# A planned order worked out anew: sigmoid attention and a gated feed-forward layer on one core

## The chip, the cores and the metric

The kernel runs on one core of a Trainium2 chip. The metric is the time of one execution on the device in microseconds (us); a comparison takes the median of several executions.

The core has five engines that run side by side: TensorE (PE in the profile) does matrix products into PSUM, ScalarE (ACT) activation functions, VectorE (DVE) elementwise work, copies and 32x32 block transposes, GpSimd (POOL) here only issues the loads, and SyncE (SP) issues the output stores. Each engine runs its own list of instructions strictly in the order in which the program wrote them, and waits at the first one whose operands or buffers are not ready.

## The reference

```python
def _attn_ref(q, k, v):                     # 8 batches, 12 heads, 448 tokens, 64 wide
    scores = scale * np.matmul(q, k.transpose(0, 1, 3, 2)) - np.log(S)
    attn = 1.0 / (1.0 + np.exp(-scores))    # a sigmoid, no softmax
    return np.matmul(attn, v).astype(np.float32)

def _moe_ref(x, w_in, w_out, beta):         # x: 3584 tokens x 768; w_in: 768 x 2048; w_out: 2048 x 768
    h = x @ w_in
    g = h * (1.0 / (1.0 + np.exp(-beta * h)))
    return (g @ w_out).astype(np.float32)
```

Attention runs per head; the heads of a batch, side by side, are the 768 columns of `x`. Inputs and output are float32; the kernel computes in float16 with float32 sums.

## The kernel before

The work is cut into **tasks**, each a few instructions of one engine. A task has a name, and the names are what the change is written in:

- **Loads (POOL queue, lines 778 to 806).** The 12 heads of a batch make three groups of four heads, 24 groups in all. `q7.0.0` and `k7.0.0` are the queries and keys of group 7 (224 KB each in SBUF) and go to one of three `raw` buffers; `v3.0` to `v3.5` are six parts of the values of batch 3 (four of 144 KB, two of 48 KB) and go to one of two `v` buffers. `wi0` to `wi7` and `wo00` to `wo11` are the weights. Loads also turn float32 into float16.
- **DVE transposes and copies.** `tq` and `tk` (L818 and L832) turn a group's raw queries and keys into `qT` and `kT` (four buffers each), and the `raw` buffer is free once they are done. `vv3` (L797) copies the two small parts of a batch's values to the other partitions.
- **Scores (PE, L845).** `h0.0.1` and the like for the first three groups, by halves of the queries; `s12.2` for group 12, key block 2. Each is followed on ACT by two sigmoids (L855) into one of ten `attn` buffers.
- **Values (PE, L867).** `a12.0.0` multiplies the sigmoids of group 12 with `v` of batch 4 (group number over three, rounded down). DVE copies the result to `xT` (L877). The last group of a batch frees its `v` buffer, and the load that takes it next waits for that: `v3.0` for `a8.0.0`, `v5.0` for `a11.0.0`, `v6.0` for `a14.0.0`, `v7.0` for `a17.0.0`; all loads behind it in `LOAD_ORDER` wait with it.
- **First layer (PE, L883).** `d3.14.0` makes 128 of the 2048 hidden columns for the 448 tokens of batch 3 in six matmuls; batch 0 does it by halves. ACT takes the sigmoid with `beta` (L892, three `sg` buffers), and DVE multiplies (`gt`, L901) and so frees the PSUM bank.
- **Second layer (PE, L1003).** `t5.3.1` is the second half of product 3 of the seven (a Strassen-like scheme) that make a pair of 128-token tiles; DVE forms sums of operands (`sum`) and adds up the results in `osb`; `z5.1` and `z5.0` (SP, L1035) store the two tiles of the pair, 384 KB each, in pieces of 96 KB for most.

What order these tasks have on their engines is worked out by the program itself before any of it is issued. `plan` (line 523) steps through time with a cost for each task. PE and POOL take their tasks in the order of two long strings, `PE_ORDER` (line 668) and `LOAD_ORDER` (line 699). DVE, ACT and SP have no such string: at line 655 the planner gives them, whenever they are free, the ready task that has been ready longest:

```python
t = min(cand, key=lambda t: (ready_at[t.i] - t.soon, t.i))
```

So a transpose stands in DVE's list at the place where the planner believed its load to be done. A load's due time is reckoned at lines 640 to 642: all loads pass one after the other through one queue at the load's own rate (195 KB/us for a whole group's queries or keys, 187 and 133 for parts of the values), 1.83 us after their issue at the earliest, and are done 0.1 us after the last byte. Stores have the fixed cost (1.7, 3.4) and are no part of that queue.

On the chip, the lists are fixed: nothing is reordered when a load comes at another time than planned. The waits between engines are semaphores.

Of the kernel before, what the change touches and what calls it, by code (L numbers as in the profile page):

```python
# [665 lines left out]


PE_ORDER = """
i0 h1.0.1 h1.0.0 h2.0.1 h2.0.0 h0.0.00 h0.0.1 h0.0.01 a1.0.0 a1.0.1 h2.1.0 a0.0.0 a0.0.1 h0.1.0 a2.0.0 a2.0.1 h0.1.1
h2.1.1 d0.9.0 d0.4.0 h1.1.1 d0.8.0 a0.1.0 h1.1.0 a2.1.0 a0.1.1 s3.1 a1.1.0 a1.1.1 s3.0 a2.1.1 d0.10.0 d0.11.0 d0.5.1  # L670
s3.2 d0.7.1 d0.2.0 d0.6.0 d0.7.0 s3.3 d0.0.1 d0.5.0 s4.1 a3.0.0 s4.2 d0.1.1 d0.2.1 d0.9.1 d0.15.0 s4.0 d0.11.1 d0.14.0
d0.1.0 d0.14.1 s4.3 d0.6.1 d0.12.0 s5.0 a4.0.0 s5.1 d0.10.1 d0.3.0 d0.13.1 s5.2 d0.12.1 d0.8.1 d0.13.0 d0.3.1 a5.0.0
d0.4.1 d0.0.0 d0.15.1 d1.6.0 d1.7.0 d1.0.0 d1.1.0 d1.10.0 d1.2.0 d1.8.0 d1.15.0 d1.12.0 d1.4.0 d1.11.0 d1.5.0 d1.14.0
t0.0.0 t0.0.1 t0.1.0 t0.1.1 t0.2.0 t0.2.1 s6.0 t0.3.0 t0.3.1 d1.9.0 s6.1 t0.4.0 d1.3.0 d1.13.0 t0.4.1 s6.2 t0.5.0
t0.5.1 t0.6.0 s6.3 t1.0.0 t1.0.1 s7.2 t0.6.1 a6.0.0 s7.0 t1.1.0 t1.1.1 t1.2.0 t1.2.1 s7.1 t1.3.0 t1.3.1 t1.4.0 t1.4.1
t1.5.0 s8.1 t1.5.1 a7.0.0 s8.0 t2.0.0 t2.0.1 t1.6.0 s8.2 t1.6.1 t2.1.0 t2.1.1 t2.2.0 t2.2.1 t2.3.0 s8.3 t2.3.1 t2.4.0
t2.4.1 t2.5.0 a8.0.0 s10.0 t2.5.1 t2.6.0 t2.6.1 s9.0 d2.1.0 d2.2.0 d2.7.0 s9.1 d2.4.0 d2.0.0 d2.3.0 s9.2 d2.5.0
d2.15.0 d2.13.0 d2.10.0 d2.12.0 d2.9.0 d2.8.0 d2.11.0 d2.6.0 d2.14.0 a9.0.0 s10.2 t3.0.0 t3.0.1 t3.1.0 s10.1 t3.1.1
t3.2.0 t3.2.1 t3.3.0 t3.3.1 t3.4.0 t3.4.1 s10.3 t3.5.0 t3.5.1 t3.6.0 t3.6.1 t4.0.0 t4.0.1 s11.1 a10.0.0 t4.1.0 t4.1.1
s11.0 t4.2.0 t4.2.1 t4.3.0 t4.3.1 s11.2 t4.4.0 t4.4.1 t4.5.0 t4.5.1 s12.2 a11.0.0 t4.6.0 s12.0 t4.6.1 d3.9.0 s12.1  # L680
d3.14.0 d3.12.0 d3.0.0 d3.10.0 s13.0 d3.8.0 d3.6.0 s12.3 d3.15.0 d3.1.0 s13.2 a12.0.0 d3.3.0 d3.5.0 d3.4.0 s13.1
d3.11.0 d3.13.0 s14.2 d3.7.0 d3.2.0 s14.1 a13.0.0 t5.0.0 t5.0.1 t5.1.0 s14.0 t5.1.1 t5.2.0 t5.2.1 t5.3.0 t5.3.1 s14.3
t5.4.0 t5.4.1 a14.0.0 s15.0 t5.5.0 t5.5.1 t5.6.0 t5.6.1 d4.2.0 d4.10.0 s15.2 d4.7.0 d4.4.0 s15.1 d4.8.0 d4.13.0 d4.6.0
s16.0 d4.12.0 a15.0.0 s17.2 d4.14.0 d4.0.0 s16.1 t6.0.0 t6.0.1 t6.1.0 s16.2 d4.3.0 d4.1.0 d4.11.0 d4.15.0 t6.1.1
d4.5.0 d4.9.0 t6.2.0 t6.2.1 t6.3.0 t6.3.1 s16.3 t6.4.0 t6.4.1 t6.5.0 t6.5.1 a16.0.0 s17.1 t7.0.0 t7.0.1 t7.1.0 t6.6.0
t6.6.1 s17.0 t7.1.1 t7.2.0 t7.2.1 t7.3.0 t7.3.1 s18.2 t7.4.0 t7.4.1 a17.0.0 s18.1 t7.5.0 t7.5.1 t7.6.0 d5.8.0 s19.0
t7.6.1 d5.14.0 s18.3 d5.15.0 d5.11.0 d5.12.0 d5.9.0 d5.4.0 s18.0 d5.0.0 d5.5.0 d5.1.0 a18.0.0 s19.2 d5.2.0 d5.13.0
s19.1 d5.7.0 d5.3.0 s20.3 d5.6.0 d5.10.0 s20.0 a19.0.0 t8.0.0 t8.0.1 t8.1.0 s20.2 t8.1.1 t8.2.0 t8.2.1 t8.3.0 t8.3.1
s20.1 t8.4.0 t8.4.1 s21.1 t8.5.0 t8.5.1 a20.0.0 s21.2 t8.6.0 t8.6.1 s22.2 d6.1.0 d6.12.0 d6.13.0 s21.0 d6.10.0 d6.0.0
d6.7.0 d6.14.0 d6.2.0 a21.0.0 s22.1 d6.6.0 d6.3.0 s22.3 d6.15.0 d6.4.0 d6.5.0 d6.9.0 s22.0 d6.8.0 t9.0.0 s23.2 a22.0.0  # L690
t9.0.1 t9.1.0 t9.1.1 t9.2.0 s23.1 t9.2.1 t9.3.0 t9.3.1 t9.4.0 t9.4.1 d6.11.0 s23.0 t9.5.0 t9.5.1 t9.6.0 t10.0.0
t10.0.1 t10.1.0 a23.0.0 t10.1.1 t10.2.0 t10.2.1 t10.3.0 t10.3.1 t10.4.0 t11.0.0 d7.2.0 t9.6.1 d7.5.0 d7.3.0 d7.10.0
t10.4.1 t10.5.0 t11.0.1 t10.5.1 t10.6.0 t10.6.1 d7.4.0 d7.1.0 d7.0.0 d7.7.0 d7.11.0 d7.6.0 t11.1.0 t11.1.1 d7.8.0
t11.2.0 d7.13.0 d7.12.0 d7.9.0 t11.2.1 t11.3.0 t11.3.1 d7.14.0 t11.4.0 d7.15.0 t11.4.1 t11.5.0 t11.5.1 t11.6.0 t11.6.1
t12.0.0 t12.0.1 t12.1.0 t12.1.1 t12.2.0 t13.0.0 t12.2.1 t13.0.1 t13.1.0 t12.3.0 t12.3.1 t13.1.1 t12.4.0 t12.4.1
t12.5.0 t12.5.1 t13.2.0 t13.2.1 t12.6.0 t13.3.0 t12.6.1 t13.3.1 t13.4.0 t13.4.1 t13.5.0 t13.5.1 t13.6.0 t13.6.1
"""
# [395 lines left out]
```

## Time and profile before

| | us |
|---|---|
| median of 3 runs | 403.95 (403.72 to 404.39) |
| the profiled execution | 401.18 |
| its span, first to last instruction | 399.4 |
| PE busy (share of the span) | 381.7 (96%) |
| ACT busy | 241.7 (61%) |
| DVE busy | 236.3 (59%) |
| POOL busy (issuing loads) | 69.1 (17%) |

The mean granted clock of TensorE is 0.972. The profiled execution ran 2.77 us shorter than the median of the timed ones, and 1.78 us of it lie outside the span.

A line of a timeline reads: start and length in us, engine, source line, operation, output and inputs, count, and in brackets how long the engine stood idle just before and what it waited for. A line of the waits reads: who waited for whom, us in total, how many times, the longest.

### The profile page before, as it was taken

To read this page: it belongs to the slowest core of one execution; us is meant where nothing else is said; L and a number is where in the kernel's file an instruction comes from. 1 tells how busy PE (TensorE), PEld (TensorE's weight loads), DVE (VectorE), ACT (ScalarE), POOL (GpSimd) and SP (SyncE) were. 2 spreads that over 40 slices of the span, in tenths; PEclk is the share of its full clock that TensorE was granted. 3 is DMA by queue.
4 is the path that set the end of the run, shared out by engine and by line. 5 is a ranking of instruction groups with operands and counts; after the bars stand their busy time and mean duration, and the time that the engine had idled before them with its cause. 6 is when DMAs were issued, how large, how long until landed. Compare 5 with 4: busy or idle time off the path is not lost.

```text
span 399.4 us, 7347 instructions
## 1 busy us (share of the span) xinstructions
PE 381.7 (96%) x2958; PEld 191.9 (48%) x2958; DVE 236.3 (59%) x456; ACT 241.7 (61%) x331; POOL 69.1 (17%) x117
## 2 busy tenths in 40 slices
PE   6899999999996999997999999988999999999996
PEld 2456765544452445442444445433444445555563
DVE  2445659995663566545587538534585445465755
ACT  1999995477645654685865874476967784135100
POOL 7845307120023000071020010070000000000000
PEclk9589999999999999998999999999999999999999
DMA  8999999655139302199054041396003000140114
GB/s 111 154 197 196 204 203 160 98 89 119 41 56 202 40 2 47 39 189 166 0 94 97 3 54 30 74 169 117 0 2 81 1 2 3 38 102 18 35 45 158
DMA packets 42289, 34.30 MB, mean 86 GB/s; under 512 B 21888, under 2 KB 38672, under 8 KB 42256
## 3 DMA queue, kind: packets, MB, share of 16 engines
q0 software_dynamic: 37008, 22.81, 41.6%
q1 hardware_dynamic: 5248, 11.02, 10.5%
q8 instruction: 23, 0.38, 0.4%
q14 instruction: 10, 0.08, 0.1%
HBM read 45.62 MB, written 11.01 MB: 142 GB/s over the span
## 4 chain that ended last, share of the span: by engine, by line
PE 84%; DMA 8%; ACT 3%; DVE 2%; issue 2%; POOL 1%; DVEq 0%; POOLq 0%
PE ps L883 33%; PE ps L1003 32%; PE ps L867 10%; PE ps L845 10%; DMA v<-in_v_dram 3%; DMA raw<-in_k_dram 3%; ACT attn L855 2%; DMA raw<-in_q_dram 2%; POOL v L789 1%; DVE gt L901 1%; DVE kT L832 0%; ACT sg L892 0%; POOL v L793 0%; DVE qT L818 0%; DVE osb L901 0%
## 5 line engine op out<-in xcount | busy, mean ns | idle before, releaser
L855 ACT ACTIVATE attn<-ps,nlogs 128x896 f16<-128x896 f32 (+1 forms) x171 | 160.0, 1002 | 61.6 <-PE ps L845 59.5
L883 PE MATMUL ps<-xT,w_in 128*128 128x448 f16 (+1 forms) x864 | 157.1, 335 | 8.6 <-DVE gt L901 8.1
L892 ACT ACTIVATE sg<-ps,beta_sb 128x448 f32<-128x448 f32 (+1 forms) x144 | 82.2, 606 | 63.6 <-PE ps L883 49.8
L883 PEld LDWEIGHTS <-w_in 128*128 128x128 f16 x864 | 82.2, 98 | 79.5 <-issue 24.7
L901 DVE TENSOR_TENSOR gt<-ps,sg 128x448 f16<-128x448 f32 (+1 forms) x144 | 78.3, 566 | 66.4 <-ACT sg L892 66.1
L1003 PEld LDWEIGHTS <-sum 128*128 128x128 f16 x560 | 52.7, 98 | 42.8 <-issue 9.1
L901 DVE TENSOR_TENSOR sum<-gt 128x1024 f16<-128x1024 f16 x70 | 47.5, 686 | 38.5 <-PE ps L1003 37.5
L1003 PE MATMUL ps<-w_T,sum 128*128 128x384 f16 x336 | 60.9, 327 | 0.0
L845 PE MATMUL ps<-qT,kT 32*128 32x448 f16 (+3 forms) x864 | 55.7, 358 | 3.7 <-DVE kT L832 2.5
L867 PE MATMUL ps<-attn,v 128*64 128x448 f16 (+3 forms) x432 | 43.9, 349 | 0.3 <-ACT attn L855 0.3
L901 DVE TENSOR_TENSOR osb<-ps,osb 128x384 f32<-128x384 f32 x70 | 38.5, 551 | 7.6 <-PE ps L1003 6.7
L1003 PE MATMUL ps<-w_out,gt 128*128 128x384 f16 x224 | 41.1, 327 | 0.0
L1003 PE MATMUL ps<-w_out,sum 128*128 128x384 f16 x224 | 40.2, 326 | 0.0
L877 DVE CAST xT<-ps 128x448 f16<-128x448 f32 (+1 forms) x54 | 28.5, 559 | 18.8 <-PE ps L867 18.7
L789 POOL DMA_DIRECT2D v<-in_v_dram x32 | 20.3, 642 | 110.1 <-PE ps L867 105.4
L867 PEld LDWEIGHTS <-v 128*64 128x64 f16 (+1 forms) x432 | 19.8, 110 | 26.9 <-issue 19.6
L845 PEld LDWEIGHTS <-kT 32*128 32x128 f16 (+1 forms) x864 | 14.8, 100 | 32.4 <-issue 27.2
L1003 PEld LDWEIGHTS <-gt 128*128 128x128 f16 x224 | 20.7, 98 | 17.6 <-issue 4.9
L778 POOL DMA_DIRECT2D raw<-in_q_dram x28 | 15.6, 565 | 59.3 <-DVE qT L818 56.6
L832 DVE STREAM_TRANSPOSE kT<-raw 128x384 f32<-128x384 f32 (+3 forms) x50 | 18.7, 388 | 11.7 <-DMA raw<-in_k_dram 11.6
L818 DVE STREAM_TRANSPOSE qT<-raw 128x448 f32<-128x448 f32 (+2 forms) x28 | 17.1, 610 | 7.5 <-DMA raw<-in_q_dram 7.5
L778 POOL DMA_DIRECT2D raw<-in_k_dram x25 | 14.0, 560 | 21.0 <-DVE kT L832 16.9
(21 smaller groups left out, 57.1 us busy)
## 6 DMA issues: line engine op xcount, KB each, us to landing
out_dram<-osb SPq DMA_DIRECT2D x98, 96.0 KB, 1.9
raw<-in_k_dram POOLq DMA_DIRECT2D x23, 224.0 KB, 6.3
raw<-in_q_dram POOLq DMA_DIRECT2D x21, 224.0 KB, 6.3
v<-in_v_dram POOLq DMA_DIRECT2D x32, 144.0 KB, 6.5
w_in<-in_moe_w_in_dram POOLq DMA_DIRECT2D x8, 384.0 KB, 9.7
w_out<-in_moe_w_out_dram POOLq DMA_DIRECT2D x4, 768.0 KB, 15.7
out_dram<-osb SPq DMA_DIRECT2D x3, 384.0 KB, 2.3
v<-in_v_dram POOLq DMA_DIRECT2D x16, 48.0 KB, 6.1
```

Of the source, the lines that this page charges most:

```text
L778: self.nc.gpsimd.dma_start(out=self.raw[slot][h0 * BLK : h1 * BLK, r, c0:c1].rearrange("p c d -> p (c d)"), in_=(self.q, self.k)[r][b, HQ ...
L789: self.nc.gpsimd.dma_start(out=to, in_=rows[:, :, JF * i * D : JF * (i + 1) * D])
L818: self.nc.vector.transpose(out=self.in_order(g, self.qT[slot][rows, c0 * BLK : c1 * BLK]), in_=self.raw[raw][rows, 0, c0:c1].rearrange("p ...
L832: self.nc.vector.transpose(out=to, in_=frm)
L845: self.nc.tensor.matmul(self.ps[base : base + nk, d + hh, u0 : u0 + n], self.kT[k][lo : lo + BLK, jt * P : jt * P + nk, e], self.qT[q][lo ...
L855: self.nc.scalar.activation(out=self.at[slot][:, :, 0:n], in_=self.ps[:, d : d + 2, 0:n], func=AF.Sigmoid, bias=self.nlogs[:, 0:1], scale= ...
L867: self.nc.tensor.matmul(self.bank(x, n)[hh * D : (hh + 1) * D], self.vs[v][base : base + nk, 2 * (s % NPAIR) + hh, jt], self.at[at][base : ...
L877: self.nc.vector.tensor_copy(out=self.xT[x][:, p, c0 : c0 + n], in_=self.bank(bank, n))
L883: self.nc.tensor.matmul(self.bank(x, n), self.w_in16[:, hc, dc * P : (dc + 1) * P], self.xT[xT][:, hc, c0 : c0 + n], start=(hc == 0), stop ...
L892: self.nc.scalar.activation(out=self.sg[slot][:, 0:n], in_=self.bank(x, n), func=AF.Sigmoid, bias=0.0, scale=self.beta_sb[:, dc : dc + 1],)
L901: self.nc.vector.tensor_tensor(out=out, in0=in0, in1=in1, op=getattr(ALU, op))
L1003: self.nc.tensor.matmul(self.bank(x, HALF), a[:, dc], w[:, dc], start=(i < 4 and dc == 0), stop=(dc == ND - 1), skip_group_check=i >= 4,)
```

## The change

Only the planner's model and the two order strings change; every task, instruction, buffer and byte stays. Three things are new in the model: a store adds its 384 KB at 183 KB/us to the same queue as the loads; a load is taken to be done not 0.1 us after its last byte but 0.3 (issued before 9 us), 1.6 (before 62 us) or 4.0 us (later); and with this model both strings are others, a permutation of the same 461 PE tasks and 113 loads.

```diff
@@ tiles
-                t = self.add("SP", f"z{p}.1", (1.7, 3.4), [ev[5], ev[3]], give=[(ev[1], "osb")])
+                t = self.add("SP", f"z{p}.1", (1.7, 3.4), [ev[5], ev[3]], give=[(ev[1], "osb")], kb=(384, 183))
...
-                t = self.add("SP", f"z{p}.0", (1.7, 3.4), [ev[6]], give=[(ev["o1"], "osb")])
+                t = self.add("SP", f"z{p}.0", (1.7, 3.4), [ev[6]], give=[(ev["o1"], "osb")], kb=(384, 183))
@@ plan
-                    done = dma_free + 0.1
+                    done = dma_free + (0.3 if now < 9 else 1.6 if now < 62 else 4.0)
...
                 done = now + t.lat
+                if t.kb:
+                    dma_free = max(dma_free, now + 1.0) + t.kb[0] / t.kb[1]
@@ PE_ORDER, the opening
-i0 h1.0.1 h1.0.0 h2.0.1 h2.0.0 h0.0.00 h0.0.1 h0.0.01 a1.0.0 a1.0.1 h2.1.0 a0.0.0 a0.0.1 h0.1.0 a2.0.0 a2.0.1 h0.1.1
+i0 h1.0.1 h2.0.1 h1.0.0 h2.0.0 h0.0.00 h0.0.1 h0.0.01 a1.0.0 a1.0.1 h0.1.0 a2.0.0 a2.0.1 h2.1.0 a0.0.0 a0.0.1 h0.1.1
...
@@ PE_ORDER, around a11.0.0 and a12.0.0
-s11.0 t4.2.0 t4.2.1 t4.3.0 t4.3.1 s11.2 t4.4.0 t4.4.1 t4.5.0 t4.5.1 s12.2 a11.0.0 t4.6.0 s12.0 t4.6.1 d3.9.0 s12.1
-d3.14.0 d3.12.0 d3.0.0 d3.10.0 s13.0 d3.8.0 d3.6.0 s12.3 d3.15.0 d3.1.0 s13.2 a12.0.0 d3.3.0 d3.5.0 d3.4.0 s13.1
+t4.1.1 s11.0 t4.2.0 t4.2.1 t4.3.0 t4.3.1 s11.2 t4.4.0 t4.4.1 t4.5.0 t4.5.1 s12.2 a11.0.0 t4.6.0 s12.0 t4.6.1 d3.9.0
+s12.1 d3.14.0 d3.12.0 d3.0.0 d3.10.0 s13.0 d3.15.0 d3.6.0 s12.3 d3.11.0 d3.4.0 d3.3.0 a12.0.0 s13.2 d3.7.0 d3.8.0
...
@@ PE_ORDER, around a17.0.0 and a18.0.0
-t6.6.1 s17.0 t7.1.1 t7.2.0 t7.2.1 t7.3.0 t7.3.1 s18.2 t7.4.0 t7.4.1 a17.0.0 s18.1 t7.5.0 t7.5.1 t7.6.0 d5.8.0 s19.0
-t7.6.1 d5.14.0 s18.3 d5.15.0 d5.11.0 d5.12.0 d5.9.0 d5.4.0 s18.0 d5.0.0 d5.5.0 d5.1.0 a18.0.0 s19.2 d5.2.0 d5.13.0
+t7.1.0 t7.1.1 s17.1 t7.2.0 t7.2.1 t7.3.0 t7.3.1 s17.0 t7.4.0 t7.4.1 t7.5.0 s18.1 a17.0.0 t7.5.1 s18.0 t7.6.0 t7.6.1
+s18.3 d5.12.0 d5.13.0 s18.2 d5.11.0 d5.15.0 d5.4.0 d5.3.0 d5.10.0 s19.0 d5.7.0 a18.0.0 s19.2 d5.8.0 d5.0.0 d5.5.0
...
@@ PE_ORDER, the end
-t12.5.0 t12.5.1 t13.2.0 t13.2.1 t12.6.0 t13.3.0 t12.6.1 t13.3.1 t13.4.0 t13.4.1 t13.5.0 t13.5.1 t13.6.0 t13.6.1
+t13.0.1 t13.1.0 t13.1.1 t12.5.1 t13.2.0 t13.2.1 t13.3.0 t13.3.1 t12.6.0 t12.6.1 t13.4.0 t13.4.1 t13.5.0 t13.5.1
+t13.6.0 t13.6.1
@@ LOAD_ORDER, whole
-v0.0 q1.0.0 k1.0.0 q2.0.0 k2.0.0 v0.1 q0.0.0 v0.5 k0.0.0 q0.0.2 k0.0.2 v0.4 v0.2 v0.3 q2.7.0 q1.7.0 q0.7.0 v1.0 wi4
-wi2 q3.0.0 wi1 k3.0.0 v1.3 wi5 wi3 q4.0.0 v1.1 k4.0.0 wi0 v1.2 v1.4 v1.5 wi7 q5.0.0 wi6 k5.0.0 wo11 wo10 wo01 wo00
-v2.0 q6.0.0 v2.3 v4.0 v2.4 q10.0.0 q9.0.0 v4.5 k6.0.0 v2.2 q7.0.0 k9.0.0 v2.1 v2.5 k10.0.0 v4.2 k7.0.0 q8.0.0 k8.0.0
-v4.3 q11.0.0 q13.0.0 v3.0 v3.1 v3.4 v3.2 k11.0.0 q12.0.0 q14.0.0 k12.0.0 v4.1 v3.3 v3.5 v5.0 k13.0.0 k14.0.0 v5.5 v5.2
-q16.0.0 k16.0.0 q17.0.0 q15.0.0 v4.4 v5.4 k15.0.0 v5.1 q23.0.0 v5.3 k17.0.0 q20.0.0 q18.0.0 k18.0.0 k20.0.0 v6.0
-q19.0.0 k19.0.0 v6.4 v6.5 q21.0.0 v7.0 v7.1 v7.2 k21.0.0 v7.5 v7.3 v6.3 v6.2 v6.1 q22.0.0 v7.4 k23.0.0 k22.0.0
+q2.0.0 q1.0.0 k1.0.0 k2.0.0 v0.0 q0.0.0 k0.0.0 k0.0.2 v0.3 v0.5 q0.0.2 v0.4 v0.1 v0.2 q0.7.0 v1.0 q2.7.0 q1.7.0 v1.2
+v1.5 wi2 wi4 q3.0.0 v1.4 k3.0.0 q4.0.0 k4.0.0 wi1 wi3 v1.3 wi5 wi0 v1.1 wi7 q5.0.0 wi6 k5.0.0 wo10 wo11 wo01 wo00
+q6.0.0 v2.0 v2.3 v2.4 v4.0 q10.0.0 q9.0.0 v2.2 k6.0.0 v4.2 v2.1 q7.0.0 k7.0.0 v4.1 v4.5 v2.5 k10.0.0 q8.0.0 k9.0.0
+k8.0.0 v3.0 v4.4 v3.1 q13.0.0 q11.0.0 v3.3 q12.0.0 v3.5 v3.4 v3.2 k11.0.0 k12.0.0 k13.0.0 v5.0 q15.0.0 k15.0.0 v5.4
+v5.3 q14.0.0 v4.3 v5.2 q16.0.0 k14.0.0 k16.0.0 q18.0.0 q17.0.0 k17.0.0 v5.1 k18.0.0 v6.0 v5.5 v6.2 q23.0.0 q20.0.0
+k20.0.0 q19.0.0 v6.1 q21.0.0 k19.0.0 v6.5 v7.0 v7.1 v6.3 v7.5 v6.4 q22.0.0 k23.0.0 v7.2 k21.0.0 v7.4 v7.3 k22.0.0
```

More of the change, by code (lines that the diff above doesn't have):

```diff
@@ L668 @@
 PE_ORDER = """
-i0 h1.0.1 h1.0.0 h2.0.1 h2.0.0 h0.0.00 h0.0.1 h0.0.01 a1.0.0 a1.0.1 h2.1.0 a0.0.0 a0.0.1 h0.1.0 a2.0.0 a2.0.1 h0.1.1
[L670 to L678, printed above, removed]
@@ L679 @@
-t3.2.0 t3.2.1 t3.3.0 t3.3.1 t3.4.0 t3.4.1 s10.3 t3.5.0 t3.5.1 t3.6.0 t3.6.1 t4.0.0 t4.0.1 s11.1 a10.0.0 t4.1.0 t4.1.1
-s11.0 t4.2.0 t4.2.1 t4.3.0 t4.3.1 s11.2 t4.4.0 t4.4.1 t4.5.0 t4.5.1 s12.2 a11.0.0 t4.6.0 s12.0 t4.6.1 d3.9.0 s12.1
-d3.14.0 d3.12.0 d3.0.0 d3.10.0 s13.0 d3.8.0 d3.6.0 s12.3 d3.15.0 d3.1.0 s13.2 a12.0.0 d3.3.0 d3.5.0 d3.4.0 s13.1
-d3.11.0 d3.13.0 s14.2 d3.7.0 d3.2.0 s14.1 a13.0.0 t5.0.0 t5.0.1 t5.1.0 s14.0 t5.1.1 t5.2.0 t5.2.1 t5.3.0 t5.3.1 s14.3
-t5.4.0 t5.4.1 a14.0.0 s15.0 t5.5.0 t5.5.1 t5.6.0 t5.6.1 d4.2.0 d4.10.0 s15.2 d4.7.0 d4.4.0 s15.1 d4.8.0 d4.13.0 d4.6.0
@@ L684 @@
-s16.0 d4.12.0 a15.0.0 s17.2 d4.14.0 d4.0.0 s16.1 t6.0.0 t6.0.1 t6.1.0 s16.2 d4.3.0 d4.1.0 d4.11.0 d4.15.0 t6.1.1
-d4.5.0 d4.9.0 t6.2.0 t6.2.1 t6.3.0 t6.3.1 s16.3 t6.4.0 t6.4.1 t6.5.0 t6.5.1 a16.0.0 s17.1 t7.0.0 t7.0.1 t7.1.0 t6.6.0
-t6.6.1 s17.0 t7.1.1 t7.2.0 t7.2.1 t7.3.0 t7.3.1 s18.2 t7.4.0 t7.4.1 a17.0.0 s18.1 t7.5.0 t7.5.1 t7.6.0 d5.8.0 s19.0
-t7.6.1 d5.14.0 s18.3 d5.15.0 d5.11.0 d5.12.0 d5.9.0 d5.4.0 s18.0 d5.0.0 d5.5.0 d5.1.0 a18.0.0 s19.2 d5.2.0 d5.13.0
-s19.1 d5.7.0 d5.3.0 s20.3 d5.6.0 d5.10.0 s20.0 a19.0.0 t8.0.0 t8.0.1 t8.1.0 s20.2 t8.1.1 t8.2.0 t8.2.1 t8.3.0 t8.3.1
@@ L689 @@
[L689 to L693, printed above, removed]
@@ L694 @@
-t11.2.0 d7.13.0 d7.12.0 d7.9.0 t11.2.1 t11.3.0 t11.3.1 d7.14.0 t11.4.0 d7.15.0 t11.4.1 t11.5.0 t11.5.1 t11.6.0 t11.6.1
-t12.0.0 t12.0.1 t12.1.0 t12.1.1 t12.2.0 t13.0.0 t12.2.1 t13.0.1 t13.1.0 t12.3.0 t12.3.1 t13.1.1 t12.4.0 t12.4.1
-t12.5.0 t12.5.1 t13.2.0 t13.2.1 t12.6.0 t13.3.0 t12.6.1 t13.3.1 t13.4.0 t13.4.1 t13.5.0 t13.5.1 t13.6.0 t13.6.1
+i0 h1.0.1 h2.0.1 h1.0.0 h2.0.0 h0.0.00 h0.0.1 h0.0.01 a1.0.0 a1.0.1 h0.1.0 a2.0.0 a2.0.1 h2.1.0 a0.0.0 a0.0.1 h0.1.1
+h2.1.1 d0.4.0 d0.9.0 h1.1.1 a2.1.0 d0.8.0 h1.1.0 a0.1.0 a0.1.1 s3.1 a1.1.0 a1.1.1 s3.2 a2.1.1 d0.5.0 d0.9.1 s3.0
@@ new lines @@
+d0.7.1 d0.5.1 d0.2.0 d0.6.0 s3.3 d0.7.0 d0.11.1 s4.2 a3.0.0 s4.1 d0.6.1 d0.10.1 d0.2.1 d0.0.1 s4.0 d0.4.1 d0.13.0
+d0.12.1 d0.10.0 d0.11.0 d0.1.0 s4.3 d0.12.0 d0.1.1 s5.0 a4.0.0 s5.2 d0.14.0 d0.3.0 s5.1 d0.14.1 d0.15.1 d0.3.1 d0.0.0
+a5.0.0 d0.8.1 d0.13.1 d0.15.0 d1.5.0 d1.11.0 d1.15.0 d1.2.0 d1.6.0 d1.1.0 d1.7.0 d1.10.0 d1.12.0 d1.3.0 d1.14.0 d1.9.0
+d1.8.0 d1.0.0 t0.0.0 t0.0.1 t0.1.0 t0.1.1 t0.2.0 t0.2.1 s6.0 t0.3.0 t0.3.1 t0.4.0 t0.4.1 t0.5.0 s6.1 t0.5.1 d1.13.0
+d1.4.0 s6.3 t0.6.0 t0.6.1 s6.2 t1.0.0 t1.0.1 t1.1.0 s7.2 a6.0.0 t1.1.1 t1.2.0 t1.2.1 s7.0 t1.3.0 t1.3.1 t1.4.0 t1.4.1
@@ new lines @@
+s7.1 t1.5.0 t1.5.1 t1.6.0 t1.6.1 s8.0 a7.0.0 t2.0.0 s8.1 t2.0.1 t2.1.0 s8.2 t2.1.1 t2.2.0 t2.2.1 t2.3.0 t2.3.1 s8.3
+t2.4.0 t2.4.1 s10.0 t2.5.0 t2.5.1 a8.0.0 s9.1 t2.6.0 t2.6.1 d2.7.0 d2.6.0 d2.8.0 d2.3.0 s9.0 d2.10.0 d2.0.0 d2.2.0
+d2.14.0 d2.9.0 d2.4.0 d2.11.0 d2.1.0 s9.2 d2.13.0 d2.5.0 d2.12.0 d2.15.0 a9.0.0 s10.2 t3.0.0 t3.0.1 t3.1.0 t3.1.1
+s10.1 t3.2.0 t3.2.1 t3.3.0 t3.3.1 t3.4.0 t3.4.1 s10.3 t3.5.0 t3.5.1 t3.6.0 t3.6.1 t4.0.0 s11.1 a10.0.0 t4.0.1 t4.1.0
+t4.1.1 s11.0 t4.2.0 t4.2.1 t4.3.0 t4.3.1 s11.2 t4.4.0 t4.4.1 t4.5.0 t4.5.1 s12.2 a11.0.0 t4.6.0 s12.0 t4.6.1 d3.9.0
@@ new lines @@
+s12.1 d3.14.0 d3.12.0 d3.0.0 d3.10.0 s13.0 d3.15.0 d3.6.0 s12.3 d3.11.0 d3.4.0 d3.3.0 a12.0.0 s13.2 d3.7.0 d3.8.0
+s13.1 d3.1.0 d3.2.0 s14.0 d3.5.0 d3.13.0 s14.1 a13.0.0 t5.0.0 t5.0.1 s14.2 t5.1.0 t5.1.1 t5.2.0 t5.2.1 t5.3.0 s14.3
+t5.3.1 t5.4.0 t5.4.1 t5.5.0 t5.5.1 s16.1 a14.0.0 t6.0.0 t6.0.1 s15.2 t5.6.0 t5.6.1 t6.1.0 t6.1.1 d4.15.0 t6.2.0 d4.7.0
+t6.2.1 t6.3.0 t6.3.1 d4.4.0 t6.4.0 t6.4.1 t6.5.0 d4.11.0 t6.5.1 s15.1 t6.6.0 t6.6.1 d4.6.0 d4.8.0 d4.1.0 d4.13.0 s15.0
+d4.2.0 d4.0.0 s16.3 a15.0.0 d4.14.0 d4.10.0 s16.2 d4.5.0 d4.12.0 s16.0 d4.9.0 d4.3.0 a16.0.0 s17.2 t7.0.0 t7.0.1
@@ new lines @@
+t7.1.0 t7.1.1 s17.1 t7.2.0 t7.2.1 t7.3.0 t7.3.1 s17.0 t7.4.0 t7.4.1 t7.5.0 s18.1 a17.0.0 t7.5.1 s18.0 t7.6.0 t7.6.1
+s18.3 d5.12.0 d5.13.0 s18.2 d5.11.0 d5.15.0 d5.4.0 d5.3.0 d5.10.0 s19.0 d5.7.0 a18.0.0 s19.2 d5.8.0 d5.0.0 d5.5.0
+s19.1 d5.1.0 d5.9.0 s20.0 d5.2.0 d5.14.0 d5.6.0 a19.0.0 s20.2 t8.0.0 t8.0.1 t8.1.0 t8.1.1 s20.3 t8.2.0 t8.2.1 t8.3.0
+t8.3.1 s20.1 t8.4.0 t8.4.1 t8.5.0 t8.5.1 s21.1 a20.0.0 t8.6.0 s21.0 t8.6.1 d6.5.0 s21.2 d6.2.0 d6.12.0 d6.1.0 s22.1
+d6.8.0 a21.0.0 s22.0 d6.10.0 d6.7.0 s22.3 d6.3.0 d6.9.0 s22.2 d6.0.0 d6.11.0 s23.1 a22.0.0 d6.15.0 s23.0 d6.14.0
@@ new lines @@
+d6.13.0 t9.0.0 d6.4.0 d6.6.0 s23.2 t9.0.1 t9.1.0 t9.1.1 t9.2.0 t10.0.0 t10.0.1 t10.1.0 a23.0.0 t9.2.1 t9.3.0 t9.3.1
+d7.1.0 t9.4.0 t9.4.1 t9.5.0 t10.1.1 t9.5.1 t10.2.0 t10.2.1 t11.0.0 t9.6.0 t9.6.1 t11.0.1 t10.3.0 t10.3.1 t10.4.0
+t10.4.1 d7.11.0 d7.13.0 t10.5.0 t10.5.1 d7.6.0 t10.6.0 t10.6.1 d7.3.0 d7.9.0 t11.1.0 t11.1.1 d7.8.0 d7.15.0 t11.2.0
+d7.10.0 t11.2.1 t11.3.0 t11.3.1 d7.7.0 t11.4.0 d7.4.0 t11.4.1 d7.0.0 d7.5.0 d7.2.0 d7.12.0 d7.14.0 t11.5.0 t11.5.1
+t11.6.0 t11.6.1 t12.0.0 t12.0.1 t12.1.0 t12.1.1 t12.2.0 t12.2.1 t12.3.0 t12.3.1 t12.4.0 t12.4.1 t12.5.0 t13.0.0
```

## The prediction

> **What bounds the kernel now.** I read the engines' shares first, then the waits of the whole span, then the timeline around each long wait, then the granted clock in those stretches.
>
> PE is busy 381.7 of 399.4 us, so the amount of matrix work, which the change leaves alone, is the floor, and only what keeps PE idle or slow can move. Below are the two largest waits of PE and the three of DVE for loads (who waited for whom; us in total, times, longest):
>
> ```profile
> DVE kT L832 <- DMA raw<-in_k_dram: 11.6, 6, 3.3
> DVE v L797 <- DMA v<-in_v_dram: 8.3, 3, 4.2
> PE ps L883 <- DVE gt L901: 8.1, 4, 3.1
> DVE qT L818 <- DMA raw<-in_q_dram: 7.5, 5, 4.1
> ...
> PE ps L845 <- DVE kT L832: 2.5, 1, 2.5
> ```
>
> PE waits four times, 8.1 us in all, for DVE's multiplications `gt`; and DVE waits for loads. The timelines join the two. Three stretches, each opened by a load of values that a finished `a` task released:
>
> ```profile
> 117.22 1.25 POOL L789 DMA_DIRECT2D v<-in_v_dram  x2 [29.46 <-PE ps L867]
> ...
> 119.12 4.70 SPq L1035 DMA_DIRECT2D out_dram<-osb  x8
> 119.66 0.59 POOL L778 DMA_DIRECT2D raw<-in_k_dram  x1
> ...
> 126.83 0.58 DVE L832 STREAM_TRANSPOSE kT<-raw 128x384 f32<-128x384 f32 x1 [3.35 <-DMA raw<-in_k_dram]
> 127.33 0.58 DVE L901 TENSOR_TENSOR gt<-ps,sg 128x448 f16<-128x448 f32 x1
> ...
> 128.63 3.74 PE L883 MATMUL ps<-xT,w_in 128*128 128x448 f16 x12 [3.07 <-DVE gt L901]
> ```
>
> ```profile
> 170.14 0.61 POOL L789 DMA_DIRECT2D v<-in_v_dram  x1 [45.74 <-PE ps L867]
> ...
> 180.29 0.65 DVE L818 STREAM_TRANSPOSE qT<-raw 128x448 f32<-128x448 f32 x1 [1.67 <-DMA raw<-in_q_dram]
> ...
> 182.53 2.40 PE L883 MATMUL ps<-xT,w_in 128*128 128x448 f16 x6 [2.33 <-DVE gt L901]
> ```
>
> ```profile
> 258.95 1.83 POOL L789 DMA_DIRECT2D v<-in_v_dram  x3 [10.16 <-PE ps L867]
> ...
> 267.06 0.70 DVE L832 STREAM_TRANSPOSE kT<-raw 128x384 f32<-128x384 f32 x2 [2.54 <-DMA raw<-in_k_dram]
> ...
> 268.32 4.70 PE L883 MATMUL ps<-xT,w_in 128*128 128x448 f16 x24 [1.49 <-DVE gt L901]
> ...
> 273.82 0.35 DVE L797 COPY v<-v 64x768 f16<-64x768 f16 x1 [2.81 <-DMA v<-in_v_dram]
> ...
> 275.94 0.73 PE L883 MATMUL ps<-xT,w_in 128*128 128x448 f16 x3 [1.17 <-DVE gt L901]
> ```
>
> In each, a transpose or copy stands at the head of DVE's list and waits for its load, the `gt` behind it are ready and can't pass, no PSUM bank comes free, and PE stops. What waits is not what PE needs: group 11's keys, at 126.83 us, are used only some 25 us later. PE lasts 2.1 us without DVE (DVE stands from 126.83 - 3.35 = 123.48, PE from 128.63 - 3.07 = 125.56).
>
> After two of these stops the matrix work also runs slower (columns: stretch and its length, then busy time of PE, PE's weight loads, DVE, ACT and POOL, the granted clock, DMA share, GB/s):
>
> ```profile
> 128.60:130.90 2.30, 2.27 (x7) 0.92 (x7) 0.51 (x1) 0.00 (x0) 0.00 (x0) 0.50 1.29 204
> ...
> 182.50:184.90 2.40, 2.37 (x14) 0.73 (x17) 1.07 (x3) 0.00 (x0) 0.56 (x1) 0.50 1.48 192
> 184.90:187.00 2.10, 2.10 (x24) 0.81 (x24) 1.01 (x3) 1.76 (x3) 0.00 (x0) 0.75 1.34 202
> ...
> 268.30:270.00 1.70, 1.68 (x9) 0.87 (x9) 0.50 (x1) 0.28 (x1) 0.30 (x1) 1.00 1.42 272
> ```
>
> **The change, part by part.** *Why DVE stands.* Its list is written by the planner's due times, so I compare these with the trace, from the release of the `v` buffer on, with the rates of the code.
> - Behind `a8`: three `v3` parts of 144 KB (0.77 us each at 187), one of 48 (0.36), `k11` (224 at 195, 1.15): 3.82 + 1.83 + 0.1 = 5.75 us. The trace: 126.83 - 117.22 = 9.61. Late by 3.86.
> - Behind `a11`, up to `q16`: 0.77 + 1.15 + 1.15 + 0.36 + 0.77 + 1.15 + 1.93 = 7.28; trace 180.29 - 170.14 = 10.15. Late by 2.87.
> - Behind `a17`, up to `k21`: 5.39 against 8.11, late by 2.72; up to `v7.4`: 10.34 against 14.87, late by 4.53.
>
> Eight stores of 96 KB lie in each stretch, 768 KB. Taking them in, the first stretch moved 704 + 768 KB in 9.61 - 1.83 us, 189 KB/us, the second 213, the third (up to `v7.4`) 178: the rates of the code, once the stores count.
>
> *Stores in the queue and slack.* In such a stretch a due time moves by 2 x 384/183 = 4.2 us for the stores and by 4.0 - 0.1 = 3.9 for the slack: 8.1 us against a lateness of 2.7 to 4.5, so 3.6 to 5.4 us are left, and 2.1 us of PE's own reserve behind them. I count all four stops as gone. The idle time is 3.07 + 2.33 + 1.49 + 1.17 = **8.06 us**. The slow clock: 24 matmuls from 268.32 to the next task at 272.96 are 0.193 us each. The 12 after the first stop took from 128.63 to 132.30, 3.67 instead of 2.32; the six after the second from 182.53 to 184.86, 2.33 instead of 1.16; the 16 scores behind them 0.90 instead of 0.53 (184.86 to 185.76 against 264.99 to 265.52). Sum 1.35 + 1.17 + 0.37 = **2.89 us**. The third and fourth stop left the clock at 1.00. What is late next is nothing that the trace shows: once DVE runs, ACT has stood idle 4.22 us before 131.06 and 3.52 us before 184.97, so PE is the bound again. If the cover fails, a stop comes back at 10.95/4 = 2.7 us each.
>
> [...]
>
> *The new strings.* Both hold the same tasks, so no DMA and no instruction is added; what moves are distances. I looked for the load behind a release with the shortest way to its user, and the tightest are two.
> - `v4.3` now stands seventh behind `v5.0`: 144 + 224 + 224 + 48 + 144 + 224 + 144 = 1152 KB, with the stores 1920, at 189 KB/us 10.2 + 1.83 = 12.0 us after `a11`. `a12` comes after two `t` halves (0.65 each), four `s` (0.52) and ten `d` (1.16): 15.0 us. 3.0 us to spare. `q15` and `q14` ahead of it need `raw` buffers, and those of groups 11 and 12 are free by then, since `s11` and `s12.2` run before `a11`.
> - `v6.4` stands fifth behind `v7.0`: 528 + 768 KB, 6.9 + 1.83 = 8.7 us after `a17`. `a18` comes after three `t`, four `s`, eight `d`: 13.3 us. The copy `vv6` (0.35) fits between.
>
> Cost 0; bounds: nothing, and one stop of 2.7 us.
>
> *The opening, to 60 us.* ACT is busy 48.42 of the 50 us from 10 to 60 and PE 47.96, both with the same work in either order. The first scores wait for `k1`, the third load in both; ahead of it and with it go 336 KB instead of 368. ACT's idle 1.6 us is all that can be won; the new slack of 1.6 instead of 0.1 us can cost one round of transposes, 1.5. I take 0, in the middle.
>
> *The end.* The last task and its store stay. `z12.0` comes six `t` halves before PE's end instead of seven, 0.65 us nearer to the last store. I take half, **+0.3 us** (bounds 0 and 0.65).
>
> **Sum**: -8.06 - 2.89 + 0.3 = -10.65. The profiled execution would go from 401.18 to 390.5. The timed runs lie 2.77 us above it; I carry the difference to the median: 403.95 - 10.65 = **393.3 us**.
>
> **The rivals.**
> - *New stops take the place of two of the four*, at `a12` or behind `a17`: 393.3 + 2 x 2.74 = 398.8. For it: a distance of 3.0 us is less than the 4.53 by which a load was late. Against: the stores are already in my 12.0 us.
> - *The slow clock is not the stops' own*, but comes with something that stays, such as loads and stores at their heaviest: 393.3 + 2.89 = 396.2. For it: two of the four stops left the clock at 1.00. Against: 0.50 begins with the first matmul behind the two longest. [...]
> - *The change doesn't do what it says*: late DVE waits are not what stops PE, and the time stays at 403.9. For it: a copy of `v` waits 4.16 us before 235.19 and PE goes on. Against: no `d` ran there, so no bank hung on DVE; at all four stops one did.
> - *Slower: `raw` buffers held longer, where DVE is full.* From 60 to 80 us DVE is busy 19.73 of 20. Transposes that stand later in its list free their buffers later, and POOL, which already waits 8.56 us for `kT` before 78.33 and 6.09 before 85.53, waits on with `v2.5` and `k8` behind it, which `a6` and `s8` need. If these 14.65 us reach PE, the time is 393.3 + 14.65 = 408; it is slower than before once more than 10.65 do. Against: `a6` comes 33.6 us behind `a5` and `s8` 43, by the same durations, and PE shows no gap from 60 to 120 us.
>
> **How the numbers follow.** My forecast 0.60, two stops left 0.16, a clock that stays slow 0.05, no effect 0.04, slower 0.15. The forecast's own range is 389 to 397.5: down by the opening's 1.6 us and by the 2.77 us, should the timed runs' excess be late loads too; up by one stop and 1.5 us in the opening. The range for 8 in 10 takes in most of the second case: 389 to 402.5. About 0.2% (0.8 us) is what a measurement of this kernel can tell from no change: faster 0.81, same 0.04, slower 0.15.
>
> **What would show it.** Right: the waits of PE for `gt` fall from 8.1 us to under 2; DVE's waits for loads after 62 us shrink from 18.8 us; the granted clock stays at 1.00 from 62 us to the end; stores and loads still overlap behind `a8`, `a11` and `a17`. The first rival shows as PE waiting for `gt` or for `v` in just those places, the last as POOL's waits for transposes growing and PE idle between 60 and 120 us. The opening is wrong if ACT's busy time from 10 to 60 us falls below 47. The forecast is wrong if the waits of PE shrink and the span doesn't.

## The result, and the profile after

The changed kernel takes 391.75 us (median of four executions, 390.86 to 392.03), the kernel before 403.84 (402.72 to 404.39): ratio 0.970, 95% interval 0.9674 to 0.9727. The forecast was 393.3 us, range 389 to 402.5. The profiled execution took 391.9 us, span 390.1, against 401.18 and 399.4.

The page of the changed kernel gives the chain that ended last, by engine:

```profile
PE 94%; ACT 3%; DMA 1%; issue 1%; DVE 1%; POOL 0%; POOLq 0%
```

DMA fell from 8% of that chain to 1%, PE rose from 84%. The waits of DVE from 62 us to the end (who waited for whom; us in total, times, longest):

```profile
DVE gt L904 <- ACT sg L895: 57.2, 59, 2.5
DVE sum L904 <- PE ps L1006: 31.4, 24, 4.1
DVE xT L880 <- PE ps L870: 16.3, 9, 5.5
DVE osb L904 <- PE ps L1006: 11.5, 14, 1.9
```

No load is among them, where 18.8 us were; and the same view for PE is empty, where `gt` stood with 8.1 us. The three places themselves, from the timeline:

```profile
119.66 5.57 SPq L1038 DMA_DIRECT2D out_dram<-osb  x8
...
120.59 0.64 POOL L792 DMA_DIRECT2D v<-in_v_dram  x1 [29.77 <-PE ps L870]
...
128.42 0.35 DVE L800 COPY v<-v 64x768 f16<-64x768 f16 x1
...
138.00 1.28 DVE L835 STREAM_TRANSPOSE kT<-raw 128x384 f32<-128x384 f32 x4
```

```profile
166.27 5.83 SPq L1038 DMA_DIRECT2D out_dram<-osb  x8
...
167.71 0.64 POOL L792 DMA_DIRECT2D v<-in_v_dram  x1 [36.35 <-PE ps L870]
...
182.88 1.64 PE L870 MATMUL ps<-attn,v 128*64 128x448 f16 x16
```

```profile
253.04 1.83 POOL L792 DMA_DIRECT2D v<-in_v_dram  x3 [8.01 <-PE ps L870]
...
262.35 0.35 DVE L800 COPY v<-v 64x768 f16<-64x768 f16 x1
...
266.60 1.64 PE L870 MATMUL ps<-attn,v 128*64 128x448 f16 x16
...
270.89 0.35 DVE L800 COPY v<-v 64x768 f16<-64x768 f16 x1
```

Stores and loads still meet behind each release (eight stores run from 254.80 us on behind the third, at 253.04), but the transposes and copies carry no bracket: DVE finds their data there. The keys of group 11, on which DVE had stood at 126.83 us, 9.6 us behind the release, are now turned in the run of four at 138.00, 17.4 us behind it. In windows (stretch and length, then busy time of PE, PE's weight loads, DVE, ACT, POOL, the granted clock, DMA share, GB/s), two of the kernel before:

```profile
10.00:60.00 50.00, 47.96 (x586) 29.46 (x578) 27.32 (x69) 48.42 (x74) 21.80 (x32) 0.88 1.35 191
...
120.00:200.00 80.00, 74.60 (x528) 33.92 (x520) 42.57 (x81) 51.31 (x68) 13.05 (x23) 0.96 0.51 85
```

and of the changed one:

```profile
10.00:60.00 50.00, 48.23 (x567) 29.06 (x568) 25.05 (x64) 46.05 (x70) 22.50 (x33) 0.80 1.37 194
60.00:120.00 60.00, 60.00 (x456) 30.61 (x453) 45.39 (x85) 37.51 (x51) 9.24 (x16) 1.00 0.50 80
120.00:200.00 80.00, 80.00 (x594) 37.61 (x591) 49.87 (x94) 55.54 (x73) 16.76 (x29) 1.00 0.58 96
...
256.00:300.00 44.00, 44.00 (x344) 19.83 (x328) 27.17 (x50) 34.16 (x46) 4.18 (x8) 1.00 0.42 74
```

From 60 us to 386, where its last matmul ends, PE is busy for all of it, with the granted clock at 1.00. The stretch from 10 to 60 us is the exception to a good result: ACT did less there than before (46.05 us against 48.42), and the stage ends later, `a5` at 62.48 us instead of 60.38 (the time at which POOL issues the load that `a5` releases). Behind `a5` the kernel went from 399.4 - 60.38 = 339.0 to 390.1 - 62.48 = 327.6 us, 11.4 us less.

### The profile page after: what moved, and what is told of

The parts are those of the page before. It is cut to its first block, busy times and chain, and to the rows that moved or that the text cites. A ratio compares the mean times of both kernels' runs of the same rounds, so it can differ in the third digit from the quotient of the medians.

```text
span 390.1 us, 7352 instructions
## 1 busy us (share of the span) xinstructions
PE 380.6 (98%) x2958; PEld 192.1 (49%) x2958; DVE 235.2 (60%) x456; ACT 242.3 (62%) x331; POOL 69.1 (18%) x117
## 4 chain that ended last, share of the span: by engine, by line
PE 94%; ACT 3%; DMA 1%; issue 1%; DVE 1%; POOL 0%; POOLq 0%
PE ps L886 39%; PE ps L1006 34%; PE ps L848 11%; PE ps L870 10%; ACT attn L858 2%; DMA raw<-in_k_dram 1%; ACT sg L895 0%; POOL raw L781 0%; DVE kT L835 0%; DVE beta_sb L775 0%; DVE osb L904 0%; POOLq L1080 0%
## 5 line engine op out<-in xcount | busy, mean ns | idle before, releaser
L870 PE MATMUL ps<-attn,v 128*64 128x448 f16 (+3 forms) x432 | 44.8, 354 | 0.2 <-ACT attn L858 0.2
L880 DVE CAST xT<-ps 128x448 f16<-128x448 f32 (+1 forms) x54 | 28.6, 561 | 26.3 <-PE ps L870 26.2
L870 PEld LDWEIGHTS <-v 128*64 128x64 f16 (+1 forms) x432 | 20.1, 112 | 27.7 <-issue 20.5
L1006 PEld LDWEIGHTS <-gt 128*128 128x128 f16 x224 | 20.9, 98 | 17.1 <-issue 4.1
L1020 ACT COPY osb<-ps 128x384 f32<-128x384 f32 x14 | 6.7, 479 | 19.1 <-PE ps L1006 18.9
## 6 DMA issues: line engine op xcount, KB each, us to landing
w_out<-in_moe_w_out_dram POOLq DMA_DIRECT2D x4, 768.0 KB, 17.1
```

The costliest lines, as they stand in the source:

```text
L870: self.nc.tensor.matmul(self.bank(x, n)[hh * D : (hh + 1) * D], self.vs[v][base : base + nk, 2 * (s % NPAIR) + hh, jt], self.at[at][base : ...
L880: self.nc.vector.tensor_copy(out=self.xT[x][:, p, c0 : c0 + n], in_=self.bank(bank, n))
L1006: self.nc.tensor.matmul(self.bank(x, HALF), a[:, dc], w[:, dc], start=(i < 4 and dc == 0), stop=(dc == ND - 1), skip_group_check=i >= 4,)
```

## The experiments

Theory A: what counts is the place of transposes and copies in DVE's list, which the planner's model sets. Its rivals are named in the expectations. The kernel before was timed beside every group of runs, and ratios are to that.

**The model without the strings.** The changed kernel with both order strings of before:

```diff
-PE_ORDER = (the new string)      LOAD_ORDER = (the new string)
+PE_ORDER = (the string of before) LOAD_ORDER = (the string of before)
```

> The new planner model (stores counted, slack) with both strings of the kernel before. TensorE's and the loads' order are those of before; only the lists of DVE, ACT and SP are written anew. Theory A (the place of transposes and copies in DVE's list is what counts): the four stops of PE go, PE's wait for gt falls from 8.1 us to under 3 us and the time to 391.5 to 397 us; one stop of up to 4 us may come where k13 has only 8.0 us to s13. Rival B (the new strings count, by the distance between a load and its user; the model was only a means to find them): the stops stay, 400 to 405 us.

392.01 us (390.19 to 394.8; ratio 0.9775, 0.9695 to 0.9855). DVE waits for no load after 62 us, and PE for `gt` not at all. The one stop is elsewhere than expected, not at `k13`:

```profile
94.51 0.59 PE L847 MATMUL ps<-qT,kT 32*64 32x448 f16 x12 [1.23 <-DVE kT L834]
```

In the order that this program works out, the lists of PE, ACT, POOL and SP are those of before, task for task; in DVE's, 32 transposes and copies of `v` stand one to eight places later, and the tasks that they let pass earlier. A stands; B falls.

**The strings without the model.** The kernel before with both new strings:

```diff
-PE_ORDER = (the string of before) LOAD_ORDER = (the string of before)
+PE_ORDER = (the new string)      LOAD_ORDER = (the new string)
```

> The new strings with the old planner model (no stores in the queue, 0.1 us of slack). Theory A: DVE's list again holds transposes and copies too early; DVE waits for loads after 62 us for 6 us or more, PE stops again once to three times, 394 to 401 us. Rival B: no stops, 391 to 393 us.

401.23 us (398.6 to 404.22; ratio 0.9987, 0.9947 to 1.0026): nothing gained, a little outside what A expected. The waits of DVE for loads are 25.5 us after 62 us:

```profile
DVE v L798 <- DMA v<-in_v_dram: 12.2, 6, 4.8
...
DVE qT L819 <- DMA raw<-in_q_dram: 8.2, 3, 3.1
DVE kT L833 <- DMA raw<-in_k_dram: 5.1, 6, 1.9
```

and in the timeline PE stops seven times, 6.7 us in all, where A expected one to three stops; behind the longest, this one, six matmuls take 2.40 us, as they did behind the second stop of the kernel before, at 0.50 (here the clock is 0.74 from 180 to 184 us and 0.83 from 184 to 188):

```profile
182.19 2.40 PE L884 MATMUL ps<-xT,w_in 128*128 128x448 f16 x6 [3.17 <-DVE gt L902]
```

With the run above this settles which half of the change works: the model, by way of DVE's list.

**Stores counted, no slack; slack, no stores counted.**

```diff
# no slack
-                    done = dma_free + (0.3 if now < 9 else 1.6 if now < 62 else 4.0)
+                    done = dma_free + 0.1
# no stores
-[ev[5], ev[3]], give=[(ev[1], "osb")], kb=(384, 183))
+[ev[5], ev[3]], give=[(ev[1], "osb")])
...
```

> New strings, stores counted, slack back to 0.1 us. The stores alone move a due time by 4.2 us behind a8, a11 and a17, against a lateness of 2.7 to 4.5 us. Theory A with the stores as the cause of the lateness: DVE waits for loads after 62 us under 3 us in all, no stop of PE over 1 us, 391 to 393.5 us. Rival C (the slack does it, the stores are not what makes loads late): several stops, 394 us and more.

> New strings, slack kept, stores not counted. The slack of 3.9 us alone covers all but 0.6 us of the largest lateness (4.53 us), and PE's reserve of 2.1 us the rest: 391 to 393 us, PE without a wait for gt. If only the stores in the queue put the transposes right: stops again, 394 us and more.

Without slack 393.97 us (392.64 to 394.96; ratio 0.9816, 0.975 to 0.9881), without stores 391.81 (390.89 to 392.32; 0.9757, 0.9684 to 0.9829). The second is as expected but for one stop of 1.1 us. The first is not: I expected DVE to wait under 3 us for loads, and its four lines sum to 18.4 us, little under the 18.8 of the kernel before:

```profile
DVE qT L821 <- DMA raw<-in_q_dram: 6.1, 4, 3.2
DVE v L800 <- DMA v<-in_v_dram: 5.9, 2, 4.4
DVE kT L835 <- DMA raw<-in_k_dram: 5.7, 5, 2.0
DVE v L800 <- DMA raw<-in_k_dram: 0.7, 1, 0.7
```

Rival C expected several stops and 394 us or more, and the run lies at that edge. Yet PE stood only 2.4 us in all, at most 0.95 at a time, and the granted clock stayed at 1.00 behind all four stops. So DVE's waits summed up say little. Its wait of 4.41 us before 260.77 us cost PE 0.27 us, and one of 3.24 us before 128.27 cost it 0.62; what a wait costs depends on PE's reserve at that place (2.1 us at the place that the prediction read it from). Against the same strings with neither term (strings without the model), counting the stores takes DVE's waits from 25.5 to 18.4 us, PE's from 6.7 to 2.4, and the time from 401.23 to 393.97. The slack alone leaves 5.0 us of DVE's waits and the one stop of PE. So the loads are late by more than the stores in the model explain; what makes up the rest is not shown.

**One load.** The kernel before, with a single due time moved:

```diff
-                    done = dma_free + 0.1
+                    done = dma_free + (6.0 if t.name == "k11.0.0" else 0.1)
```

> The kernel before, with the planner's due time of a single load, k11.0.0, 6.0 us later instead of 0.1; both strings as before. Only DVE's list moves: the transposes of k11 stand five tasks later. Theory A (each stop is the late load at the head of DVE's list, on its own): the first stop goes, 3.07 us idle and 1.35 us of slow clock, so 4.4 us less than before, and the other stops stay. Rival E (the stops come from the burst of loads and stores as a whole, and a later load takes the first stop's place): within 1.5 us of before.

397.44 us against 402.73 (ratio 0.9878, 0.9845 to 0.9911), 5.3 us less by the medians, 4.9 by the ratio; the 4.4 expected, a ratio of 0.9891, lie in the interval. The timeline holds the other three stops, each in its place some 5 us earlier, and no first:

```profile
128.49 6.80 PE L883 MATMUL ps<-xT,w_in 128*128 128x448 f16 x35
...
129.29 0.69 DVE L832 STREAM_TRANSPOSE kT<-raw 128x384 f32<-128x384 f32 x2
```

```profile
178.08 1.30 PE L883 MATMUL ps<-xT,w_in 128*128 128x448 f16 x6 [2.20 <-DVE gt L901]
262.83 4.70 PE L883 MATMUL ps<-xT,w_in 128*128 128x448 f16 x24 [1.99 <-DVE gt L901]
270.22 2.43 PE L883 MATMUL ps<-xT,w_in 128*128 128x448 f16 x12 [0.95 <-DVE gt L901]
```

In the order that this program works out only DVE's list differs: the two transposes of group 11 stand five and four places later, and behind them the two of group 12 and a copy of `v` four to six. These five tasks were worth about 1% of the kernel. The first stop was the late load at the head of DVE's list, and it could go without the others; that each of the other three is as separate was not tested by a run of its own, and rests on the timeline.

**The opening.** To find where the 2.1 us of the opening went, the old opening in the changed kernel, and both kernels profiled once more:

```diff
-                    done = dma_free + (0.3 if now < 9 else 1.6 if now < 62 else 4.0)
+                    done = dma_free + (0.1 if now < 62 else 4.0)
# and both strings as before up to a5.0.0 and wo00
```

> The changed kernel with the strings of before up to a5.0.0 and up to wo00 and with 0.1 us of slack in the opening; the new strings and model behind that. Theory F (the 2.1 us by which the changed kernel's opening was longer in its profile, 62.48 against 60.38 us to the end of a5, come from when the granted clock returns to 1.00, which differs from run to run): the time stays at 391 to 392.5 us. Rival G (they come from the new order of the opening): 389.5 us, and the profile has a5 end at 60.4 us.

> The kernel before once more, for a second profile. Theory F: the granted clock returns to 1.00 at another time between 20 and 30 us, and the end of a5 moves with it by up to 2.5 us, while the stops behind 120 us are there again. Rival G: a5 ends at 60.4 us again.

> The changed kernel once more, for a second profile. Theory F: the end of a5 moves with the clock's return, somewhere from 60 to 62.7 us. Rival G: 62.5 us again. Either way no wait of PE for gt and no wait of DVE for a load after 62 us.

The old opening gives 393.26 us (392.39 to 394.23; ratio 0.9776, 0.9732 to 0.982): no gain, so G falls, though it lies 0.8 us above what F expected. The stretch from `a5` to the end is 1.4 us longer than the changed kernel's (329.1 against 327.7), with one wait of PE, 0.9 us; whether the old opening costs anything beyond noise is not settled (ratios of the changed kernel 0.970 and 0.9743). The kernel before, again: 401.38 us, `a5` at 62.11; the changed one: 392.14, `a5` at 62.71. The granted clock in windows of 2 us gives the times of its fall and its return. Windows away from a change show 0.50 or 1.00, so a window at 0.85 behind others at 0.50 is read as at 1.00 for 70% of it. Over the runs:

| run | clock falls, us | is back, us | at 0.50 for, us | end of `a5`, us | from there to the end, us |
|---|---|---|---|---|---|
| before | 8.4 | 22.1 | 13.6 | 60.38 | 339.0 |
| no slack | 9.4 | 23.1 | 13.7 | 60.08 | 331.2 |
| old opening | 11.0 | 28.0 | 17.1 | 61.55 | 329.1 |
| changed, third profile | 11.3 | 28.4 | 17.1 | 61.55 | 327.7 |
| before, again | 8.1 | 28.6 | 20.5 | 62.11 | 337.5 |
| changed | 9.6 | 30.0 | 20.5 | 62.48 | 327.6 |
| changed, again | 10.7 | 31.2 | 20.5 | 62.71 | 327.6 |

The end of `a5` goes with the clock's return, for old and new order alike (the kernel before has the first and the fifth row; no slack has the new strings and the shortest opening). Six more profiles agree: with the clock back at 22.9 and 24.9 us (one load, strings without the model) `a5` ends at 60.59 and 61.23, and with the clock back at 29.0 to 30.8 us at 61.70 to 62.67. The stretches come in steps of 3.4 us: four, five or six of them. That the clock is the cause of the 2.1 us is the reading that fits all rows; no run set the clock by itself.

**More empty matmuls, and twice the slack.** Two edits of the changed kernel, timed beside it:

```diff
# more idle
-        for i, n in enumerate((14,)):
+        for i, n in enumerate((22,)):
# slack 8
-                    done = dma_free + (0.3 if now < 9 else 1.6 if now < 62 else 4.0)
+                    done = dma_free + (0.3 if now < 9 else 1.6 if now < 62 else 8.0)
```

> The changed kernel, timed beside the next two on the same chip: 391 to 392.5 us.

> The changed kernel with 22 instead of 14 empty matmuls at the start, which fill most of the gap of PE before its first scores. Theory H (the clock falls in the opening because PE pauses before its first scores): the granted clock stays above 0.5 from 10 to 20 us, a5 ends at 60.5 us or before, 389 to 390.5 us. Rival J (it falls because the scores of the opening leave PE too little to do): the clock is at 0.50 by 14 us as before, and the time within 0.8 us of the changed kernel.

> The changed kernel with 8.0 us of slack after 62 us instead of 4.0. The transposes move further back in DVE's list, and raw buffers are held longer. Theory A (once no load is late, more slack changes nothing, as DVE's list still keeps the transposes ahead of their users): within 1 us of the changed kernel. Rival D (raw buffers held longer make POOL and then PE wait; the rival on the other side of the prediction): PE waits for kT or attn after 62 us, 394 us and more.

The changed kernel: 391.42 us (ratio 0.9743, 0.9711 to 0.9775). More idle: 391.76 (0.9741, 0.9713 to 0.977); the clock falls at 13.4 us instead of 11.3 and is back at 30.5, five steps of 3.4 us again, so the pause before the first scores (PE busy 0.01 us of the 2 from 6 to 8 us in the changed kernel, 2.00 here) isn't what holds it down. H falls; the time and the clock are as J has them, but its reason, that the scores leave PE too little to do, was not tested. Slack of 8: 398.24 us (0.9903, 0.9874 to 0.9932), 6.8 us more, where A expected less than 1. DVE waits for no load here either. The timeline of PE has one long stop, and DVE's shows why:

```profile
92.07 0.63 DVE L821 STREAM_TRANSPOSE qT<-raw 128x448 f32<-128x448 f32 x1
92.63 1.25 DVE L904 TENSOR_TENSOR sum<-gt 128x1024 f16<-128x1024 f16 x2
93.80 0.70 DVE L835 STREAM_TRANSPOSE kT<-raw 128x384 f32<-128x384 f32 x2
```

```profile
94.55 0.96 PE L848 MATMUL ps<-qT,kT 32*64 32x448 f16 x12 [3.46 <-DVE kT L835]
```

PE needs the last keys of group 7 at 91.1 us (94.55 - 3.46), and their transpose stands behind two `gt` and two sums. The data were there: the transpose carries no bracket, and in the changed kernel the same load is issued at nearly the same time (80.97 us against 81.29) and turned at 88.40, also without a wait. So rival D has the time and the wait for `kT` right, but not its reason. From 93.8 to 100.6 us the clock is at 0.50 (0.91 from 90.7 to 94.5 us, 0.84 from 100 to 102), two steps; of these PE works from 94.55 on, 6.05 us at half speed, which is 3.0 us lost. With PE's waits, 3.46 and another of 0.48, that makes 7.0 us for the 6.8 measured. To see whether it is this one place:

```diff
-                    done = dma_free + (0.3 if now < 9 else 1.6 if now < 62 else 8.0)
+                    done = dma_free + (0.3 if now < 9 else 1.6 if now < 62 else 4.0 if t.name in ("q7.0.0", "k7.0.0") else 8.0)
```

> As with 8.0 us of slack, but the loads of group 7 alone keep 4.0. The run with 8.0 us for all lost 6.8 us against the changed kernel and shows one long stop, 3.46 us at 94.55 us, where PE waits for the last transpose of group 7. Theory K (that stop alone, with the slow clock behind it, is the loss: a transpose too late in DVE's list for its user): 391 to 392.5 us, no wait of PE over 1 us there. Rival L (the loss is spread over all the later places): 396 us and more.

392.34 us (390.97 to 392.94; ratio 0.9749, 0.9712 to 0.9787), with a single wait of PE of 0.5 us. K stands: the loss was one transpose too late in the list, the mirror image of the stops before.

## Why the prediction was right

*The four stops.* As predicted, all went, with the slow clock behind them (1.00 from 60 to 386 us), and nothing took their place. The sum said 10.65 us less; behind `a5` it was 11.4 between the two profiles, or 9.9 from the second profile of before (337.5 to 327.6), since the stops themselves differ from run to run. One number by the way was misread: the keys of group 11, turned at 126.83 us, are first used at 158.09 (`s11.1`, just ahead of `a10`), 31 us later and not 25, which only makes the case stronger.

*How near the median came.* The 1.6 us between 393.3 and 391.75 are in part luck. The opening took 2.1 us more than the sum had, the part behind it 0.75 less, and the 2.77 us of excess that the forecast carried along are -0.15 in the changed kernel (391.75 against its profile's 391.9): errors of +2.1, -0.75 and -2.9 that cancel in part.

*The slow clock, 2.89 us.* Right in the profile at hand, but not a fixed price: the first stop cost 1.35 us of it there and none in the second profile of before, where PE stood 2.13 us and the clock was at 1.00 behind it (129.4 to 131.8 us). There the second stop, 2.17 us, halved the clock (0.52 from 182.1 to 184.5 us), and the third, 2.30, didn't (1.00 from 268.8 to 271 us). In the first profile of before the slow stretch behind the first stop ran from 127.9 to 131.3 us, by the windows' shares (0.95 from 127 to 128 us, 0.50 up to 131, 0.84 from 131 to 132), one step of 3.4 us like those of the opening. So the length of a stop did not settle by itself whether the clock fell: 2.17 us were enough, 2.30 were not. What settles it, no run shows.

*Due times.* That the stores explain the lateness is borne out only in part: with them counted and no slack, DVE still waited 18.4 us for loads. Both terms together, 8.1 us, are more than is needed: the slack alone does (391.81 us), and the stores alone come near (393.97).

*The strings, cost 0.* Right: alone they change nothing that can be told (ratio 0.9987, 0.9947 to 1.0026). The distances held: `a12` began 15.2 us behind the release by `a11` (182.88 - 167.71) for 15.0 worked out, and waited for nothing.

*The opening, 0 with bounds of -1.6 and +1.5.* Wrong in the profile: +2.1 us, outside both bounds, and the sign that I had named for it, ACT busy under 47 us, is there (46.05). But the sign doesn't tell the orders apart: the run with both old strings in the new model has it too (45.88). The step left out the clock, which I took as given; it is back anywhere from 22 to 31 us, with the old order as with the new. Among profiles with the same stretch at 0.50 the order of the strings makes at most 0.9 us: `a5` ends at 60.38 and 60.59 us with the old and 60.08 and 61.23 with the new (13.6 us at 0.50), at 62.11 and 62.67 with the old and 62.48 and 62.71 with the new (20.5 us). So for the order itself a term of 0 was near.

*The end, +0.3.* From PE's last matmul to the end it was 3.9 us (399.4 - 395.5) and is 4.05 (390.1 - 386.05): +0.1.

*The 2.77 us* by which the timed runs of before exceeded its profile were carried along as they were. The profile of before had the early clock, and the timed runs of before spread over 399.2 to 405.7 us, those of the changed kernel over 390.8 to 393.0. I take it that part of that excess was the openings and stops of other executions, and that it went with the stops; no profile shows those executions.

*The rivals.* None came true. What was said against the third, that no `d` ran while a copy of `v` waited 4.16 us before 235.19, was misread: PE ran four `d` from 232.71 us on (24 matmuls in 4.71 us, without a stop) while DVE stood from 231.03. The `d` began 2.48 us before DVE went on, near the reserve of 2.1 us read elsewhere; that this is why nothing stopped is my reading, not shown. The rival on the other side, transposes later in the list where DVE is full, is real, and lies only four microseconds of slack further on: at 8.0 us it costs 6.8, at the stage that I had named, though by the list and not by the `raw` buffers.

## What to carry to other kernels

In a list that an engine runs strictly in order, a step that waits for a transfer has a window: not before the data surely lands, not behind what its user can spare. Here a planner that was optimistic about loads by 2.7 to 4.5 us cost 3% of the time, while another order of the large work alone changed nothing that can be told. So measure its due times against the trace, place by place, and add the slack there. Don't add up an engine's waits; compare each with the reserve that the engine behind it has.
